# An attention and bilinear-FFN kernel: GpSimd copies patterns by 64-bit additions, VectorE takes the norm multiplications and 175 key tiles, and the order is planned anew

## The chip, the cores and the metric

One core of a Trainium2 chip. Its engines run their own instruction queues: TensorE (PE, with its weight loads listed as PEld), VectorE (DVE), ScalarE (ACT), GpSimd (POOL), and SyncE (SP), which here only starts DMA transfers. They meet through semaphores. Everything one engine does is in program order on that engine.

The metric is the device time of the program in microseconds (us), one launch on one core. The kernel before takes 706.86 us, the median of three runs between 705.78 and 707.62.

## What is computed

Two branches over the same 2048 rows of 512 values, mixed row by row by a sigmoid gate:

```python
def _A_ref(x, wqkv, wo):            # S = 2048, D = 512, H = 32 heads, Dh = 16
    qkv = (x @ wqkv).reshape(B, S, 3, H, Dh).transpose(2, 0, 3, 1, 4)
    q, k, v = qkv[0], qkv[1], qkv[2]
    scores = einsum("bhqd,bhkd->bhqk", q, k) * (Dh ** -0.5)
    p = softmax(scores, axis=-1)
    o = einsum("bhqk,bhkd->bhqd", p, v)
    return o.transpose(0, 2, 1, 3).reshape(B, S, D) @ wo

def _B_ref(x, w_gate, w_up, w_down):     # F = 1376
    return ((x @ w_gate) * (x @ w_up)) @ w_down

g = sigmoid((x * gate_w).sum(-1, keepdims=True))
out = g * _A_ref(x, ...) + (1 - g) * _B_ref(x, ...)
```

The heavy part is the softmax: 32 heads x 2048 x 2048 exponentials, 134 million.

## The kernel before

**Tiles.** The queries are cut into four chunks of 512, the heads into groups of eight. A "quad" is four heads with one chunk of queries: 32 quads, taken one after the other. For each quad there are 16 key tiles of 128 keys, so 512 steps in all. A step has four score tiles, each 128 keys by 512 queries, one PSUM bank each. Each bank is made by four matmuls that use one half of the PE array (64 rows) and a quarter of its columns each; the two halves work side by side (`scores` and `pe64`, L1621, where every such matmul is recorded). The banks then go one of two ways.

- An **A step**: ACT takes the exponential of a bank, or of two neighbouring banks in one instruction, and writes bf16 weights to SBUF cells (`exp`, L1721). Then 8 matmuls multiply the four cells with the values (`pv`).
- A **D step**: VectorE approximates the exponential. One addition and a clamp per bank turn the scaled score into a 16-bit integer whose bits, read as bf16, are a piecewise-linear power of two (`dpass`, L1757). To average out the error of that shape there are four patterns: the integers themselves and three copies with 32, 64 and 96 added (`copy`, L1763 on VectorE, L1767 on GpSimd). Each pattern is multiplied with the values scaled by 2^(-v/4), prepared by `v_scale`, so that a D step has 32 value matmuls and not 8. A copy is 128 x 2048 16-bit numbers, or half of that.

Six of the 16 key tiles of a quad (`dks`) may be D steps; 150 of the 512 steps are.

**Value sums and norm.** All value matmuls of a quad add up in PSUM bank 7; a seventeenth column of ones gives the denominators. At the end of a quad VectorE moves the bank out, scaled by a row of gate factors (L1833). For each pair of quads the denominators are gathered by a DMA, inverted (`recip`, L1847), written to DRAM and read back broadcast to all rows (`rbc`, L1918). A multiplication on GpSimd, `mult` (L1926), then gives the normed block. 16 of these are recorded.

**Filling.** The projections for keys, values and queries, the FFN (`u_copy`, `g_mul`) and the output projection are cut into units of a few matmuls on one bank and put between the attention steps.

**The order.** Nothing in the order is left to a run-time scheduler. `_Sched` is a planner that plays the program through with its own durations for each instruction and appends each instruction to its engine's list as it chooses it. In `try_act`, `try_dve`, `try_pool` and `pe_phase` it asks a set of knobs (`PAR`), each a table over planned time with an entry per 4 us: how many score banks may be out, when ACT waits for a neighbouring bank, when GpSimd and when VectorE copies. `_Plan.emit` then writes the lists out, with a semaphore wait wherever an instruction needs another engine's result. The planner lets VectorE's copies and GpSimd's instructions exclude each other (`lock_v`, `dve4_until`), and a GpSimd copy also waits for the last of VectorE's (`last4`).

**Buffers.** The patterns live in eight buffers `DB` and, after their first use as weights, in `wv` and `wk`; the ACT cells in `PT`, and later in `xT`, `wd`, `wu`, `wg`, `hT` and `wo` as these come free.

Of the kernel before, what the change touches and what calls it, by code (L numbers as in the profile page):

```python
# [10 lines left out]
I32 = mybir.dt.int32  # L11
# [126 lines left out]
class _Sched:  # L138
# [582 lines left out]
    def try_act(self):  # L721
# [27 lines left out]
        if grp is not None and self.cfree[grp]:  # L749
            n = 1  # L750
            if len(self.cfree[grp]) > 1:
                for i in range(len(rd)):
                    j = next((j for j in range(i + 1, len(rd)) if abs(rd[j][4] - rd[i][4]) == 1), None)
                    if j is not None and (i == 0 or self.g("apick")):
                        x, y = rd[i], rd[j]
                        rd.remove(x)
                        rd.remove(y)
                        rd[:0] = [x, y]
                        n = 2
                        break  # L760
                if n == 1 and o == 2:
                    n = 0
                if n == 1 and o != 1 and any(abs(x[4] - rd[0][4]) == 1 and x[0] <= self.now + self.g("await") for x in self.aready):
                    n = 0
        for x in rd[n:]:
            heapq.heappush(self.aready, x)
        if n == 0:
            return False
        rd = rd[:n]
        cells = [self.cfree[grp].pop(0) for _ in range(n)]  # L770
# [27 lines left out]


# [5 lines left out]
    def try_dve(self):  # L805
# [18 lines left out]
        for x in self.small:  # L824
            if x[0] <= now:
# [3 lines left out]
                return True  # L829
        c4 = self.lock_v <= now  # L830
# [102 lines left out]
    def cp_done(self, e, v, hs, op, t):  # L933
# [6 lines left out]
        if not e.cptodo:  # L940
            self.cpq.remove(e)
        if st[5] == 2:
# [30 lines left out]
    def try_pool(self):  # L973
# [5 lines left out]
        for x in self.ptask:  # L979
            if x[0] <= now:  # L980
                self.ptask.remove(x)
                self.log("pool", x[1], x[3])
                self.pool_v = self.lock_v = self.now + x[1]
                self.at(self.pool_v)
                x[2]()
                return True
        if self.dve4_until + 0.063 > now:
            return False
        if self.accq and self.accq[0][2] <= now:
            self.acc_pool()  # L990
            return True
        for e in self.cpq:
# [127 lines left out]
    def norm1(self, m, op):  # L1120
# [48 lines left out]
    def norm2(self, bi):  # L1169
# [21 lines left out]
    def norm3(self, bi, o):  # L1191
        c, b = divmod(bi, 4)
        op = self.hw.mult(bi, [o] + self.dep([("x", ch) for ch in range(1, min(self.par["xq"], 2) + 1)]) + self.rdep(("ocb", bi)) + [self.last4] + self.rdep(("outl", c - 2))) if self.hw else None
        self.setr(("ot", bi), self.now + 1.27 + 0.05 + 0.05, op)
# [261 lines left out]
    def run(self):  # L1456
# [29 lines left out]
        self.oev, self.fev, self.small, self.cpq, self.scale4, self.ptask = [], [], [], [], [], []  # L1486
# [63 lines left out]
class _Hw:  # L1550
# [6 lines left out]
    def __init__(self, nc, stack, par, A_x, A_wqkv, A_wo, W_gate, W_up, W_down, gate_w, out):  # L1557
# [42 lines left out]
        self.cadd = sb("cadd", [128, 4, 2], I16)  # L1600
# [111 lines left out]
    def exp(self, banks, cells, deps):  # L1712
        g, i = cells[0]
        t = self.grp[g]
        if len(banks) == 2:
            s = cells[1][1] - i
            dst = t[:, i : cells[1][1] + 1 : s, :]
            src = self.ps[:, banks[0] : banks[1] + 1, :]
# [40 lines left out]
    def copy(self, eng, src, dst, v, hs, deps):  # L1759
        lo, hi = 1024 * hs[0], 1024 * hs[-1] + 1024  # L1760
        a, o = self.db[src][:, lo:hi], self.db[dst][:, lo:hi]
        if eng == "dve":
            return self.dve(lambda e: e.tensor_scalar(o, a, 32.0 * v, None, ALU.add), deps)  # L1763
        n = (hi - lo) // 2
        return self.P.op(
            "pool",
            lambda e: e.tensor_tensor(o.bitcast(I32), a.bitcast(I32), self.cadd[:, v, :].bitcast(I32).to_broadcast([128, n]), ALU.add),  # L1767
            deps + [self.r["cadd"]],
        )
# [144 lines left out]

    def rbc(self, bi, deps):
# [9 lines left out]
    def mult(self, bi, deps):  # L1925
        return self.P.op("pool", lambda g: g.tensor_tensor(self.OT[:, bi % 8, :], self.oc[:], self.rb[:], ALU.mult), deps)  # L1926


    def prologue(self):
# [55 lines left out]
        for v in range(1, 4):  # L1985
            ca = pool(lambda g, v=v: g.memset(self.cadd[:, v, :], 32.0 * v))
# [60 lines left out]
        r["cadd"] = ca  # L2047
        r["qmz"] = qz2
        if self.par["acc"]:
# [9 lines left out]
 'ND': 8,  # L2059
 'acc': 0,  # L2060
# [3 lines left out]
 'alook': ((13, 2), (5, 6), (8, 4), (6, 2), (9, 6), (6, 2), (3, 4), (8, 2), (2, 6), (2, 5), (3, 6), (6, 5),  # L2064
           (4, 2), (3, 5), (15, 2), (3, 6), (5, 2), (7, 6), (2, 2), (15, 6), (3, 3), (24, 2), (12, 6), (6, 2),
           (10, 5)),
 'alook2': ((8, 4), (5, 3), (1, 4), (3, 6), (1, 4), (5, 3), (9, 0), (5, 5), (21, 4), (10, 6), (10, 4), (2, 3),
            (3, 0), (8, 4), (1, 6), (3, 5), (9, 6), (6, 4), (18, 5), (21, 4), (6, 5), (9, 0), (16, 6)),
 'amax': ((7, 5), (157, 4), (6, 5), (10, 4)),
 'amin': ((7, 3), (1, 2), (7, 3), (5, 2), (3, 3), (2, 2), (1, 4), (6, 2), (6, 4), (3, 3), (3, 4), (13, 2),  # L2070
          (2, 4), (9, 3), (10, 2), (2, 4), (13, 2), (8, 4), (9, 2), (18, 4), (25, 2), (5, 4), (6, 3), (6, 2),
          (10, 3)),
 'apick': ((11, 0), (17, 1), (52, 0), (3, 1), (6, 0), (17, 1), (55, 0), (3, 1), (16, 0)),
 'ares': ((14, 1), (9, 2), (9, 1), (5, 2), (1, 1), (3, 2), (3, 0), (14, 1), (10, 0), (10, 2), (2, 1), (11, 2),
          (13, 1), (6, 0), (15, 2), (15, 0), (15, 2), (15, 1), (10, 0)),
 'await': ((2, 0.05), (10, 0), (6, 0.05), (5, 0), (3, 0.2), (6, 0.1), (5, 0.2), (1, 0), (3, 0.05), (3, 0),
           (12, 0.05), (2, 0), (1, 0.1), (3, 0.4), (6, 0), (10, 0.05), (2, 0), (3, 0.2), (6, 0.05), (5, 0.1),
           (16, 0), (18, 0.2), (12, 0), (6, 0.05), (3, 0.2), (9, 0.05), (6, 0.4), (6, 0.2), (10, 0.4)),
 'cpmax': ((2, 10), (12, 6), (3, 4), (6, 6), (8, 5), (1, 8), (5, 14), (1, 5), (3, 8), (3, 14), (3, 8),
           (11, 14), (6, 3), (7, 14), (4, 5), (3, 14), (2, 10), (3, 8), (8, 5), (4, 6), (45, 14), (10, 5),  # L2080
           (3, 14), (2, 10), (6, 14), (3, 8), (3, 5), (3, 10), (10, 3)),
 'dact': ((13, 2), (24, 3), (4, 2), (3, 3), (14, 2), (79, 3), (8, 2), (19, 3), (6, 1), (10, 3)),
 'dahead': ((2, 0), (56, 1), (10, 0), (21, 1), (5, 0), (73, 1), (13, 0)),
 'dend': ((2, 2), (3, 3), (2, 1), (10, 0), (20, 3), (4, 5), (3, 0), (6, 2), (18, 4), (3, 3), (4, 4), (3, 3),
          (2, 0), (12, 4), (3, 0), (15, 2), (3, 5), (6, 3), (3, 5), (3, 0), (3, 3), (12, 2), (3, 3), (9, 4),
          (6, 3), (6, 4), (6, 2), (10, 4)),
 'dks': [2, 4, 7, 9, 12, 14],
# [3 lines left out]
 'dlook': ((29, 1), (8, 2), (7, 1), (6, 0), (51, 1), (4, 2), (5, 1), (18, 2), (24, 1), (6, 2), (3, 1), (3, 2),  # L2091
           (16, 1)),
 'dlook2': ((2, 0), (6, 1), (11, 0), (4, 3), (9, 2), (3, 4), (6, 1), (6, 3), (11, 2), (10, 3), (12, 0),
            (3, 3), (8, 0), (5, 3), (8, 2), (6, 3), (3, 4), (6, 1), (9, 4), (12, 3), (13, 0), (1, 3), (3, 4),
            (1, 0), (12, 1), (10, 3)),
 'dmaq': 2.0,
 'dmax': ((5, 2), (3, 3), (24, 2), (12, 3), (6, 2), (30, 3), (3, 2), (8, 3), (10, 2), (79, 3)),
 'dpair': ((8, 1), (3, 2), (17, 0), (1, 1), (3, 2), (9, 0), (27, 1), (3, 2), (9, 0), (3, 1), (11, 0), (1, 2),
           (15, 1), (15, 0), (3, 2), (12, 1), (18, 0), (6, 2), (16, 1)),
 'dpri': ((21, 1), (29, 0), (9, 1), (105, 0), (6, 1), (10, 0)),  # L2100
 'dresv': ((8, 0), (5, 3), (79, 0), (9, 1), (79, 0)),
 'dwait': ((2, 0.4), (3, 0), (20, 0.2), (1, 0.1), (6, 0.2), (5, 0.4), (1, 0.2), (3, 0), (3, 0.1), (11, 0),
           (10, 0.1), (3, 0.4), (9, 0.2), (3, 0.1), (11, 0.2), (4, 0), (15, 0.1), (18, 0.4), (9, 0.1),
           (9, 0.2), (6, 0.1), (6, 0), (6, 0.4), (6, 0), (10, 0.1)),
 'fcf': ((7, 1), (173, 0)),
 'fdebt': ((2, 0), (9, -10), (3, 25), (3, 0), (11, 25), (2, 0), (2, -30), (5, 25), (1, 0), (3, -30), (17, 25),
           (2, 10), (11, 0), (7, 25), (2, 0), (3, -30), (8, 25), (1, 0), (14, -30), (4, 25), (3, 10), (6, 25),
           (6, 10), (15, 25), (8, 0), (7, 25), (9, 0), (6, -30), (10, 0)),
 'ffn0': 2.6,
 'ffn1': 31.5,  # L2110
 'flead': ((2, 160), (3, 40), (6, 160), (6, 10), (12, 0), (9, 80), (3, 160), (12, 10), (9, 160), (4, 20),
           (2, 40), (3, 10), (9, 80), (3, 40), (8, 80), (1, 160), (9, 10), (9, 20), (18, 80), (9, 20), (3, 0),
           (5, 20), (8, 80), (1, 160), (1, 80), (9, 0), (6, 80), (10, 160)),
 'fmax': ((41, 3), (17, 1), (8, 2), (5, 3), (9, 2), (3, 3), (8, 2), (19, 1), (18, 3), (14, 1), (11, 2),
          (11, 3), (6, 1), (10, 2)),
# [116 lines left out]
```

## Time and profile before

| what | value |
|---|---|
| median of three runs | 706.86 us (705.78 to 707.62) |
| span of the profiled execution | 702.0 us |
| granted clock of TensorE, mean | 0.999 |
| PE busy, matmuls | 688.9 us, 22,151 |
| ACT busy | 681.2 us |
| DVE busy | 652.3 us |
| POOL busy | 460.4 us |
| HBM traffic | 20 GB/s over the span |

The profiled execution is told by its span, from the first to the last instruction; the runs' times also hold what lies before and after. A busy time is the union of an engine's instructions. An instruction's record begins before the one ahead of it has ended, since each engine overlaps the end of one with the start of the next, so the price of an instruction in a full queue is the step from its start to the next one's. A matmul is 0.38 us long in the record, while eight are under way at a time. The listing of a group gives line, engine, operation, output and inputs with shapes, then count, busy time, mean duration, and the idle time of the engine just before, with what ended it.

### The profile page before, as it was taken

The page shows a single profiled execution, that of the slowest core. Times are in us where ns is not written, and L with a number is a line of the kernel's source. Part 1 is how long each engine was busy: PE and PEld are TensorE (multiplying, and loading weights), DVE is VectorE, ACT ScalarE, POOL GpSimd, SP SyncE. Part 2 cuts the span into 40 slices and gives each one's busy share as a digit, 9 for nine tenths or more (in the row PEclk, how much of TensorE's full clock was granted, in tenths as well). Part 3 has the DMA queues.
Part 4 walks back from the last instruction along what each step waited for, and adds up shares of the span by engine and source line. Part 5 has one row for each costly group of instructions (what it writes and reads, how often), then busy time and mean ns, then how long its engine had stood idle before and what let it go on. Part 6 is the DMA issues. An engine that isn't in the chain of part 4 may idle for free.

```text
span 702.0 us, 47197 instructions
## 1 busy us (share of the span) xinstructions
PE 688.9 (98%) x22151; PEld 370.6 (53%) x22151; DVE 652.3 (93%) x1063; ACT 681.2 (97%) x839; POOL 460.4 (66%) x328
## 2 busy tenths in 40 slices
PE   8999999999999999999999999999999999999997
PEld 4565555455444545555544555555554555555564
DVE  5899999999999999999999999899999988999986
ACT  5899999999999999999999999999999999999995
POOL 3348877777765657777675566777776576768711
PEclk9999999999999999999999999999999999999999
DMA  7301341103010100001000010100101010010101
GB/s 153 74 4 47 97 100 28 14 13 101 17 29 12 43 12 21 28 12 28 14 21 20 21 33 19 35 13 12 29 5 42 13 36 22 10 29 19 30 20 34
DMA packets 33748, 22.94 MB, mean 33 GB/s; under 512 B 19500, under 2 KB 30156, under 8 KB 33552
## 3 DMA queue, kind: packets, MB, share of 16 engines
q1 hardware_dynamic: 32416, 18.86, 10.9%
q8 instruction: 173, 2.83, 1.7%
q0 software_dynamic: 176, 0.53, 0.3%
q10 hardware_dynamic: 960, 0.52, 0.3%
q14 instruction: 23, 0.19, 0.1%
HBM read 11.71 MB, written 2.36 MB: 20 GB/s over the span
## 4 chain that ended last, share of the span: by engine, by line
PE 71%; ACT 26%; DVE 1%; DMA 1%; issue 0%; ACTq 0%; DVEq 0%
PE ps L1621 70%; ACT PT L1721 16%; ACT xT L1721 8%; ACT wd L1721 2%; DMA DB<-in_A_x_dram 1%; ACT wu L1721 1%; DVE DB L1757 0%; DVE hT L1905 0%; ACT wg L1721 0%; PE ps L2020 0%; DVE oraw L1833 0%; DVE wv L1757 0%; ACTq L1936 0%; ACT QM L2033 0%; DVEq L88 0%
## 5 line engine op out<-in xcount | busy, mean ns | idle before, releaser
L1621 PE MATMUL ps<-QM,KT 64*32 64x512 bf16 x8192 | 497.2, 379 | 3.4 <-ACT wd L1721 0.8
L1721 ACT ACTIVATE PT<-ps 128x1024 bf16<-128x1024 f32 (+1 forms) x449 | 404.3, 1049 | 1.8 <-PE ps L1621 1.8
L1767 POOL TENSOR_TENSOR DB<-DB,cadd 128x1024 int32<-128x1024 int32 (+1 forms) x186 | 279.0, 1519 | 141.5 <-DVE DB L1763 56.2
L1757 DVE TENSOR_SCALAR DB<-ps 128x512 int16<-128x512 f32 (+1 forms) x457 | 304.8, 694 | 21.8 <-PE ps L1621 16.7
L1621 PE MATMUL ps<-DB,Vs 64*17 64x512 bf16 x3024 | 275.6, 377 | 0.5 <-issue 0.3
L1621 PEld LDWEIGHTS ps<-QM,KT 64*32 64x32 bf16 x8192 | 155.0, 90 | 162.5 <-ACT PT L1721 51.1
L1621 PE MATMUL ps<-PT,Vp 64*17 64x512 bf16 x1638 | 227.5, 377 | 0.2
L1721 ACT ACTIVATE xT<-ps 128x1024 bf16<-128x1024 f32 (+1 forms) x232 | 211.4, 1028 | 0.9 <-PE ps L1621 0.8
L1621 PE MATMUL ps<-xT,Vp 64*17 64x512 bf16 x822 | 145.9, 377 | 0.1
L1621 PE MATMUL ps<-xT,wu 64*32 64x512 bf16 x1376 | 110.5, 377 | 0.0
L1621 PE MATMUL ps<-xT,wg 64*32 64x512 bf16 x1376 | 108.2, 377 | 0.0
L1621 PE MATMUL ps<-wd,hT 64*32 64x512 bf16 x1408 | 102.2, 377 | 0.0
L1763 DVE TENSOR_SCALAR DB<-DB 128x2048 int16<-128x2048 int16 (+1 forms) x140 | 95.9, 714 | 0.5 <-PE ps L1621 0.2
L1621 PEld LDWEIGHTS ps<-DB,Vs 64*17 64x17 bf16 x3024 | 74.1, 87 | 34.0 <-PE ps L1621 5.1
L1621 PE MATMUL ps<-DB,Vp 64*17 64x512 bf16 x928 | 89.7, 377 | 0.8 <-DVE oraw L1833 0.3
L1621 PEld LDWEIGHTS ps<-PT,Vp 64*17 64x17 bf16 x1638 | 56.6, 87 | 21.0 <-PE ps L1621 7.2
L1721 ACT ACTIVATE wd<-ps 128x1024 bf16<-128x1024 f32 (+1 forms) x73 | 66.1, 1058 | 0.0
L1767 POOL TENSOR_TENSOR DB<-wv,cadd 128x512 int32<-128x512 int32 (+1 forms) x35 | 50.0, 1452 | 21.6 <-PE ps L1621 15.3
L1757 DVE TENSOR_SCALAR wv<-ps 128x512 int16<-128x512 f32 (+1 forms) x78 | 52.7, 699 | 2.5 <-PE ps L1621 1.7
L1621 PEld LDWEIGHTS ps<-wd,hT 64*32 64x32 bf16 x1408 | 36.8, 92 | 13.0 <-issue 1.2
L1621 PEld LDWEIGHTS ps<-xT,wu 64*32 64x32 bf16 x1376 | 35.5, 92 | 13.3 <-DVE DB L1757 1.0
L1621 PEld LDWEIGHTS ps<-xT,wg 64*32 64x32 bf16 x1376 | 34.8, 92 | 13.5 <-DVE DB L1757 1.3
(108 smaller groups left out, 890.9 us busy)
## 6 DMA issues: line engine op xcount, KB each, us to landing
rb<-rscr SPq DMA_DIRECT2D x16, 256.0 KB
QM<-qraw SPq DMA_DIRECT2D x124, 16.0 KB, 2.2
oc<-oraw SPq DMA_DIRECT2D x60, 32.0 KB, 2.3
out_dram<-ost SPq DMA_DIRECT2D x12, 128.0 KB, 2.2
wd<-in_B_w_down_dram SPq DMA_DIRECT2D x10, 128.0 KB, 2.3
wu<-in_B_w_up_dram SPq DMA_DIRECT2D x12, 96.0 KB, 3.1
wg<-in_B_w_gate_dram SPq DMA_DIRECT2D x12, 96.0 KB, 2.1
wv<-in_A_wqkv_dram POOLq DMA_DIRECT2D x1, 512.0 KB, 4.8
```

Source lines behind the costliest of these rows:

```text
L1621: o = pe.matmul(dst, lhs, rhs, start=st, stop=sp, tile_position=(64 * r, 32 * cc), skip_group_check=True)
L1721: return self.P.op("act", lambda a: a.activation(dst, src, ACT.Exp, scale=self.ES), deps)
L1757: return self.dve(lambda v: v.tensor_scalar(dst, src, self.YB, 0.0, ALU.add, ALU.max), deps)
L1763: return self.dve(lambda e: e.tensor_scalar(o, a, 32.0 * v, None, ALU.add), deps)
L1767: lambda e: e.tensor_tensor(o.bitcast(I32), a.bitcast(I32), self.cadd[:, v, :].bitcast(I32).to_broadcast([128, n]), ALU.add),
```

## The change

- GpSimd's copies: `copy` for "pool" was a 32-bit tensor addition with a constant tile `cadd`, broadcast, as second operand. It becomes `int64_add` with an immediate, 0x0020002000200020 times v, over the same bytes seen as 64-bit integers. `cadd` and its three memsets go. The operation belongs to another GpSimd code library than the one loaded at the start, and the program's listing has a load of it ahead of the first copy. A new function `turn`, a GpSimd addition over the small `mask` tile, is issued when the last copy is planned; ahead of it the first library is loaded again.
- The norm multiplication `mult` goes from GpSimd to VectorE. In the planner it has a queue of its own, `mq`, looked at after the small tasks and before the copies and passes; it counts as an instruction that excludes GpSimd's, as VectorE's copies do.
- The planner may give ACT three banks at equal distances of cells in one instruction (`three`, knob `a3`), and charges other durations: a GpSimd copy 1.02 and half a copy 0.593, where it had 1.849 and 0.997; the reciprocal 0.27, where it had 0.58.
- All knob tables are new. In the listing this makes 175 D steps (150 before), 1037 exponentials over one bank, 154 over two and one over three (204, 622 and none before), 55 whole copies and one half on VectorE (219 and 12), 415 whole and 109 half copies on GpSimd (156 and 138), and 22,751 matmuls (22,151).

```diff
+        if self.mq and self.mq[0][0] <= now:
+            x = self.mq.pop(0)
+            dur = 0.602 + max(0.0, self.lock_v - self.now)
+            self.dve_go(dur, ("M", x[1]))
+            self.dve4_until = self.dve_v + 0.165
+            (self.at(self.dve4_until), self.at(self.dve4_until + 0.063))
+            self.norm3(x[1], x[2], dur)
+            return True
...
         if not e.cptodo:
             self.cpq.remove(e)
+            if self.hw and self.qd >= self.NG and all(x.npass == 4 and not x.cptodo for x in self.dsteps[-6:]):
+                self.hw.turn()
...
             if both and bl >= self.g("gfull"):
-                hs, dur = [0, 1], 1.849
+                hs, dur = [0, 1], 1.02
             elif bl >= self.g("ghalf"):
-                hs, dur = [h], 0.997
+                hs, dur = [h], 0.593
...
-                self.small.append((t + self.par["rmarg"], 0.58, lambda: self.norm2(bi), ("R", bi)))
+                self.small.append((t + self.par["rmarg"], 0.27, lambda: self.norm2(bi), ("R", bi)))
...
-                    self.ptask.append((t2 + self.par["mmarg"], 1.27, lambda: self.norm3(bi, o2), ("M", bi)))
+                    self.mq.append((t2 + self.par["mmarg"], bi, o2))
...
-        n = (hi - lo) // 2
-        return self.P.op(
-            "pool",
-            lambda e: e.tensor_tensor(o.bitcast(I32), a.bitcast(I32), self.cadd[:, v, :].bitcast(I32).to_broadcast([128, n]), ALU.add),
-            deps + [self.r["cadd"]],
-        )
+        return self.P.op("pool", lambda e: e.int64_add(o.bitcast(I64), a.bitcast(I64), 0x0020002000200020 * v), deps)
...
+    def turn(self):
+        return self.P.op("pool", lambda g: g.tensor_tensor(self.mask[:], self.mask[:], self.mask[:], ALU.add), [self.r["q"], self.r["q0b"]])
...
     def mult(self, bi, deps):
-        return self.P.op("pool", lambda g: g.tensor_tensor(self.OT[:, bi % 8, :], self.oc[:], self.rb[:], ALU.mult), deps)
+        return self.dve(lambda v: v.tensor_tensor(self.OT[:, bi % 8, :], self.oc[:], self.rb[:], ALU.mult), deps)
...
-        for v in range(1, 4):
-            ca = pool(lambda g, v=v: g.memset(self.cadd[:, v, :], 32.0 * v))
...
 PAR = {'NA': 14,
  'ND': 8,
+ 'a3': ((4, -1), (2, 0.1), (6, -1), (2, 0.1), (1, 0.4), (2, -1), (2, 0.1), (1, 0.05), (11, -1), (1, 0.05), (5, 0),
...
- 'await': ((2, 0.05), (10, 0), (6, 0.05), (5, 0), (3, 0.2), (6, 0.1), (5, 0.2), (1, 0), (3, 0.05), (3, 0),
...
+ 'await': ((3, 0.05), (1, 0), (2, 0.1), (2, 0.05), (1, 0.1), (2, 0.2), (6, 0), (2, 0.05), (26, 0), (2, 0.1), (3, 0),
...
```

More of the change, by code (lines that the diff above doesn't have):

```diff
@@ L10 @@
 I16 = mybir.dt.int16
-I32 = mybir.dt.int32
+I64 = mybir.dt.int64
 ACT = mybir.ActivationFunctionType
@@ L764, in try_act @@
                     n = 0
+        cells = None
+        a3 = self.g("a3")
+        if n == 2 and a3 >= 0:
+            lo = min(rd[0][4], rd[1][4])
+            cells = self.three()
+            if cells:
+                j = next((j for j in range(2, len(rd)) if rd[j][4] in (lo - 1, lo + 2)), None)
+                if j is not None:
+                    rd.insert(2, rd.pop(j))
+                    n = 3
+                elif any(x[4] in (lo - 1, lo + 2) and x[0] <= self.now + a3 for x in self.aready):
+                    n = 0
+                else:
+                    cells = None
+        if n == 0:
+            for x in rd:
+                heapq.heappush(self.aready, x)
+            return False
         for x in rd[n:]:
             heapq.heappush(self.aready, x)
-        if n == 0:
-            return False
         rd = rd[:n]
-        cells = [self.cfree[grp].pop(0) for _ in range(n)]
+        if n == 3:
+            for x in cells:
+                self.cfree[x[0]].remove(x)
+        else:
+            cells = [self.cfree[grp].pop(0) for _ in range(n)]
         cells.sort()
@@ L797, in try_act, with three @@
         return True
+    def three(self):
+        for gi in (8, 9, 10, 1, 2, 7, 6, 5, 4, 3, 0):
+            f = self.cfree[gi]
+            if len(f) < 3:
+                continue
+            c = sorted(x[1] for x in f)
+            for i in range(len(c) - 2):
+                for j in range(i + 1, len(c) - 1):
+                    if 2 * c[j] - c[i] in c:
+                        return [(gi, c[i]), (gi, c[j]), (gi, 2 * c[j] - c[i])]
+        return None
     def dve_go(self, dur, what):
@@ L1189, in norm2, with norm3 @@
         self.at(t, go)
-    def norm3(self, bi, o):
+    def norm3(self, bi, o, dur):
         c, b = divmod(bi, 4)
-        op = self.hw.mult(bi, [o] + self.dep([("x", ch) for ch in range(1, min(self.par["xq"], 2) + 1)]) + self.rdep(("ocb", bi)) + [self.last4] + self.rdep(("outl", c - 2))) if self.hw else None
-        self.setr(("ot", bi), self.now + 1.27 + 0.05 + 0.05, op)
+        op = self.hw.mult(bi, [o] + self.dep([("x", ch) for ch in range(1, min(self.par["xq"], 2) + 1)]) + self.rdep(("ocb", bi)) + self.rdep(("outl", c - 2))) if self.hw else None
+        self.last4 = op
+        self.setr(("ot", bi), self.now + dur + self.DEND + 0.05, op)
     def simple(self, dur, dend, key, make, after=None):
@@ L1485, in run @@
         self.dma_v = 0.0
-        self.oev, self.fev, self.small, self.cpq, self.scale4, self.ptask = [], [], [], [], [], []
+        self.oev, self.fev, self.small, self.cpq, self.scale4, self.mq = [], [], [], [], [], []
         self.fact, self.fnext, self.fdone = [], 0, 0
@@ L1714, in exp @@
         t = self.grp[g]
-        if len(banks) == 2:
+        if len(banks) > 1:
             s = cells[1][1] - i
-            dst = t[:, i : cells[1][1] + 1 : s, :]
-            src = self.ps[:, banks[0] : banks[1] + 1, :]
+            dst = t[:, i : cells[-1][1] + 1 : s, :]
+            src = self.ps[:, banks[0] : banks[-1] + 1, :]
         else:
@@ L2046, in prologue @@
         r["er1"] = er1
-        r["cadd"] = ca
         r["qmz"] = qz2
@@ new lines @@
+ 'fmax': ((12, 3), (2, 2), (1, 3), (8, 2), (6, 3), (9, 2), (1, 3), (2, 1), (1, 2), (8, 1), (13, 3), (1, 2), (19, 3),
+          (1, 1), (2, 3), (3, 2), (21, 3), (5, 2), (3, 3), (1, 1), (2, 2), (1, 1), (1, 3), (1, 1), (4, 3), (1, 1),
+          (1, 2), (1, 1), (25, 3), (6, 1), (1, 3), (2, 1)),
+ 'fres': ((130, 0), (1, 1), (30, 0), (1, 2), (1, 0), (1, 1), (1, 0)),
+ 'fs2': ((10, 1), (2, 0), (2, 1), (5, 0), (1, 1), (6, 0), (5, 1), (7, 0), (89, 1), (1, 0), (12, 1), (1, 0), (17, 1),
+         (5, 0), (2, 1)),
@@ L2135 @@
+ 'gwin': ((1, 0), (3, 0.5), (2, 0), (3, 0.5), (2, 0), (1, 0.8), (2, 0), (5, 0.2), (7, 0.8), (3, 1.2), (2, 0.2),
[5 rows of a table added]
  'hold': 1,
```

140 lines of the change are left out of this document (58 added, 82 removed), and 67 rows, old and new, of the table PAR.

## The prediction

> **What bounds the kernel now.** I read the page's first and fourth parts, then the groups by form, the waits, the stages and the timeline. The page:
>
> ```profile
> span 702.0 us, 47197 instructions
> PE 688.9 (98%) x22151; PEld 370.6 (53%) x22151; DVE 652.3 (93%) x1063; ACT 681.2 (97%) x839; POOL 460.4 (66%) x328
> ...
> PE 71%; ACT 26%; DVE 1%; DMA 1%; issue 0%; ACTq 0%; DVEq 0%
> ...
> L1721 ACT ACTIVATE PT<-ps 128x1024 bf16<-128x1024 f32 (+1 forms) x449 | 404.3, 1049 | 1.8 <-PE ps L1621 1.8
> ```
>
> Three engines are over 90% busy and the chain changes between PE and ACT, so busy shares don't say which one binds. An instruction's busy time also overlaps the next one's, so I price by the step between starts. The timeline (start, length, engine and group):
>
> ```profile
> 304.05 0.64 ACT L1721 ACTIVATE xT<-ps 128x512 bf16<-128x512 f32 x1
> 304.53 1.76 ACT L1721 ACTIVATE PT<-ps 128x512 bf16<-128x512 f32 x3
> ...
> 328.32 4.80 ACT L1721 ACTIVATE PT<-ps 128x1024 bf16<-128x1024 f32 x5
> 332.90 2.05 ACT L1721 ACTIVATE xT<-ps 128x1024 bf16<-128x1024 f32 x2
> ```
>
> An exponential over one bank takes 0.48 us, one over two banks 4.58/5 = 0.916. The program before lists 204 and 622 of them: 97.9 + 569.8 = 667.7 us. They run from 9.57 (the chain) to 692.0 (the stages of line 1721 alone):
>
> ```profile
> 9.57 3.35 ACT wu L1721 x4
> ```
>
> ```profile
> 10.00:692.00 682.00, 673.73 (x826) 1.00 0.12 30
> 692.00:702.00 10.00, 0.00 (x0) 0.91 0.16 54
> ```
>
> So ACT works 667.7 of 682.4 us, 97.8%, and loses 14.7 us: ACT is the bound. PE has room. The stages, with the number of matmuls behind each busy time:
>
> ```profile
> core 0: us, PE busy (x) PEld busy (x) DVE busy (x) ACT busy (x) POOL busy (x), PEclk, DMA share, GB/s
> 0.00:20.00 20.00, 17.14 (x327) 9.62 (x327) 12.19 (x26) 12.44 (x19) 6.52 (x15) 1.00 0.77 145
> ...
> 60.00:160.00 100.00, 98.78 (x3216) 51.80 (x3208) 94.47 (x153) 99.64 (x114) 77.21 (x45) 1.00 0.22 52
> 160.00:260.00 100.00, 99.51 (x3032) 48.95 (x3023) 96.81 (x156) 99.41 (x123) 65.11 (x57) 1.00 0.13 36
> ...
> 560.00:660.00 100.00, 99.59 (x3388) 57.52 (x3384) 94.22 (x147) 99.45 (x116) 72.36 (x49) 1.00 0.08 22
> ```
>
> A PE "99% busy" does 3032 matmuls in one stage and 3388 in another: 33.0 and 29.5 ns each. Four matmuls on one half of the array start every 0.215 us when nothing holds them:
>
> ```profile
> 687.82 0.39 PE L1621 MATMUL ps<-wd,hT 64*32 64x512 bf16 x4
> 688.03 0.39 PE L1621 MATMUL ps<-wd,hT 64*32 64x512 bf16 x4
> 688.25 0.39 PE L1621 MATMUL ps<-wd,hT 64*32 64x512 bf16 x4
> ```
>
> With both halves that is 0.215/8 = 26.9 ns each. What holds PE is mostly ACT, which frees the score banks (the waits):
>
> ```profile
> PEld ps L1621 <- ACT PT L1721: 51.7, 207, 0.8
> ...
> PEld ps L1621 <- ACT xT L1721: 26.9, 112, 0.5
> ...
> PEld ps L1621 <- DVE DB L1757: 16.0, 70, 0.6
> ```
>
> **The change, part by part.** Counts are from the listings of the two programs, durations from the profiled execution.
>
> *25 more key tiles on VectorE (150 to 175 of 512).* ACT loses 100 of 1448 banks. The new order however takes few in pairs: 1037 of one bank, 154 of two, one of three. Cost 497.8 + 141.1 + 1.4 = 640.3 us (the three-bank one as two steps), 27.4 less than now.
>
> PE gets 24 matmuls per tile, 600: 22,151 to 22,751. At today's 31.1 ns (0.1 ms stage, x3216) that would be 18.7 us if PE bound; beside ACT it costs nothing while PE can run denser than it does.
>
> *Pattern copies.* 450 become 525. VectorE made 219 whole and 12 half, now 55 and one half; GpSimd 156 whole and 138 half, now 415 and 109. Their rows, and what else GpSimd's durations depend on:
>
> ```profile
> L1767 POOL TENSOR_TENSOR DB<-DB,cadd 128x1024 int32<-128x1024 int32 x105 | 196.8, 1891 | 96.7 <-DVE DB L1763 39.5 <-PE ps L1621 31.2 <-DVE DB L1757 17.0
> ...
> L1767 POOL TENSOR_TENSOR DB<-DB,cadd 128x512 int32<-128x512 int32 x81 | 82.3, 1037 | 44.8 <-DVE DB L1763 16.7 <-PE ps L1621 14.5 <-DVE wv L1763 7.4
> ```
>
> ```profile
> 2.27 0.52 POOL L1960 MEMSET erow<- 128x512 f32 x1
> 2.73 0.95 POOL L1961 MEMSET QM<- 128x1024 bf16 x1
> ...
> 20.89 3.74 POOL L1767 TENSOR_TENSOR DB<-DB,cadd 128x1024 int32<-128x1024 int32 x2 [11.66 <-DVE DB L1757]
> ```
>
> No row has a 64-bit addition. A whole copy is 1024 words of 32 bits, or 512 of 64. If elements count it costs what 512 do, 1.04; if bytes count, 1.89; if one operand instead of two is what matters, down to the memset's 0.52. The memsets, of 2 KB both, take 0.52 and 0.95 for 512 and 1024 elements, so elements count: I take 1.04 whole and, with 0.85 us per 512 elements (1.89 - 1.04), 0.61 half. GpSimd then works 415 x 1.04 + 109 x 0.61 = 498 us, 74% of the forecast's 669; it stays off the path, and a pattern is ready sooner.
>
> The Trainium skill (GPSIMD Engine Reference, section 3.1) has two-input bodies at about 2.6 cycles per element and small one-input bodies at 1.03, with a 1.2 GHz clock. 1024 words at 1.03 cycles would be an estimated 0.88 us plus dispatch, close to the 1.04 I take; the sum would not move.
>
> *VectorE.* Its steps:
>
> ```profile
> 318.90 1.28 DVE L1763 TENSOR_SCALAR DB<-DB 128x2048 int16<-128x2048 int16 x2
> 320.10 0.35 DVE L1847 RECIPROCAL rec<-den 128x32 f32<-128x32 f32 x1
> ...
> 323.18 1.28 DVE L1757 TENSOR_SCALAR wv<-ps 128x512 int16<-128x512 f32 x2
> 324.38 1.29 DVE L1763 TENSOR_SCALAR DB<-DB 128x2048 int16<-128x2048 int16 x2
> ```
>
> ```profile
> L1757 DVE TENSOR_SCALAR DB<-ps 128x1024 int16<-128x1024 f32 x7 | 8.5, 1219 | 1.0 <-PE ps L1621 0.8
> ...
> L1763 DVE TENSOR_SCALAR DB<-DB 128x1024 int16<-128x1024 int16 x3 | 1.3, 419 | 0.0
> ```
>
> Both a score pass and a whole copy take 0.60 (two in 1.20, start to start). Passes go from 582 (and 9 double, 1.2) to 692 (and 4): +60 us. Copies go from 219 to 55, and 11 of 12 halves (0.42 at most) go: -103 us. The 16 norm multiplications come over from GpSimd:
>
> ```profile
> L1926 POOL TENSOR_TENSOR OT<-oc,rb 128x512 bf16<-128x512 f32 x16 | 20.5, 1279 | 28.2 <-DVE DB L1763 28.2
> ...
> L1882 DVE TENSOR_TENSOR OT<-oraw,rb 128x256 bf16<-128x256 f32 x2 | 0.8, 424 | 0.3 <-ACT rb L1881 0.3
> ```
>
> The half-size form takes 0.42 on VectorE, so 0.42 to 0.85 whole; with 0.60 that is 9.6 us. Together VectorE does 33 us less. The multiplication reads two SBUF tiles; if VectorE must wait out a GpSimd copy each time, 16 x 1.04 = 16.6 us come back, still under today's load. What is new is a wait in VectorE's queue for the broadcast reciprocals (line 1947, by DMA). Behind it stand score passes of 0.6 us each, and PE waits for the banks they free. Before, GpSimd waited for that transfer once:
>
> ```profile
> POOL DB L1767 <- DMA rb<-rscr: 2.0, 1, 2.0
> ```
>
> Bounds: 0 to 16 x 2.0 = 32 us. I take 0, nearest to one in sixteen, since the 28.2 us in which GpSimd's multiplications waited for VectorE show the reciprocals lying ready.
>
> *Two library loads on GpSimd* (the 64-bit addition lives in another one; the dummy addition of `turn` brings the first back). The one at the start is hidden by the 11.66 us before the first copy. The other falls into the idle before the tail's only GpSimd instruction:
>
> ```profile
> 697.95 1.26 POOL L1902 TENSOR_TENSOR hT<-oc,wu 128x512 bf16<-128x512 f32 x1 [10.30 <-DVE hT L1905]
> ```
>
> I price both at nothing; without that cover the first patterns come late, and PE's queue, in order, stands behind them. The `cadd` memsets and their dependency go, inside the same idle time. SP issues the same 370 instructions, in a new order; its transfers are cheap (a DMA share of 0.22 from 60 to 160 us, 0.13 from 160 to 260).
>
> **The sum.** Before the first exponential 9.6 us, after the last 10.0: both prologue and tail keep their work. Exponentials 640.3. ACT's loss is unknown: 0 if the order feeds it without a hole, and up to what PE's density sets. The chain's last matmuls:
>
> ```profile
> 696.64 0.48 PE ps L1621 x8
> ```
>
> At the best stage's 29.5 ns PE needs (22,751 - 327) x 29.5 = 661.5 us from 20.0 on, and 4.9 us follow its last matmul: 686.4. So the span lies between 659.9 and 686.4. Today's loss of 14.7 us would become 14.4 if it goes with the time ACT works (2.2% of 654.7), and 3.6 if it arises where two banks must be ready together (154 doubles for 622). A fuller PE speaks for the first, the single banks for the second; I take the middle, 9.0: 9.6 + 640.3 + 9.0 + 10.0 = 668.9. The median of the runs (706.86) is 4.9 us over the profiled span (702.0), which I add unchanged: 674.
>
> **The rivals.**
> PE becomes the bound at its best density: 686.4 + 4.9 = 691, faster. For it speaks that the forecast needs 28.7 ns for 644 us ((668.9 - 4.9 - 20.0)/22,424), which no stage reached; against it, that PE waits 79 us for ACT's banks, the very work that shrinks.
> PE can't run denser than on average: at 31.1 ns its 22,424 matmuls take 697.4 us, 722.3 + 4.9 = 727, slower. It decides from 30.2 ns ((702.0 - 24.9)/22,424). The stage at 29.5 speaks against it.
> The 64-bit addition costs by bytes, so that the change doesn't do what it says: 415 x 1.89 + 109 x 1.04 = 898 us on GpSimd alone, with 21 before and about 15 behind it 934 + 4.9 = 939, slower. From some 1.4 us a copy GpSimd's 667 us are full. The memsets speak against it.
> The library load isn't hidden: it begins only with the first copy. Should it last as long as the whole idle stretch, all behind it moves by 11.7: 686. The Trainium skill (GPSIMD Engine Reference, section 2.1) puts the first call after a load at about 6 us, which no row here shows; by it the time would be an estimated 680 without cover.
>
> **How the numbers follow.** Forecast 0.62 (own range 665 to 686), PE at its best density 0.21, the load 0.04; slower: PE's mean density 0.06, bytes 0.04. The 0.03 left is for the others' neighbourhood within 0.3%, about what a measurement of this kernel tells from no change. Faster 0.87, same 0.03, slower 0.10. The range goes from 662, the span's lower bound of 659.9 with half of the 4.9, to 694, past the second case.
>
> **What would show it.** Right: GpSimd's new group at about 1.04 us per whole copy and under 80% busy; ACT's step at 0.48 and its exponentials ending some 10 us before the end; matmuls at 3450 or more per 100 us; fewer PE waits for ACT. Wrong: PE waits for GpSimd's copies as their longest entry, VectorE idle for the reciprocals' DMA, stages of 3200 matmuls, or an idle GpSimd stretch behind the first data.

## The result and the profile after

The changed kernel takes 697.77 us, the median of four runs between 695.81 and 700.59; the kernel before, in the same session, 707.24. The ratio is 0.988 (0.9847 to 0.9914): 1.2% faster, where 674 us, 4.6%, was forecast. The profiled execution took 700.59 us with a span of 698.8. Ratios, here and below, leave disturbed runs out; medians and ranges keep them.

The page of the changed kernel (busy time by engine; the queue of instruction fetches; the chain that ended last; GpSimd's new group as count, busy, mean ns, idle before and its releaser):

```profile
span 698.8 us, 48944 instructions
PE 680.9 (97%) x22751; PEld 391.3 (56%) x22751; DVE 618.4 (88%) x1009; ACT 671.2 (96%) x1205; POOL 498.4 (71%) x540
...
q8 instruction: 178, 2.92, 1.8%
...
PE 93%; ACT 3%; issue 2%; DMA 1%; POOL 0%; DVE 0%; SPq 0%; DVEq 0%
...
L1795 POOL INT64_ADD DB<-DB x350 | 327.4, 949 | 146.7 <-PE ps L1652 76.7
```

The chain says it first. ACT had 26% of it and PE 71%; now PE has 93%. VectorE is 34 us less busy, and GpSimd works 498 us. The forecast had the same 498, but for the copies alone; they take 488.8, and 9.8 go to GpSimd's other instructions, so that the match is luck. All that was meant to become lighter on ACT and VectorE did. The stages of the changed kernel, with the number of matmuls behind PE's busy time:

```profile
60.00:160.00 100.00, 98.00 (x3302) 56.78 (x3294) 91.71 (x150) 97.53 (x179) 82.94 (x97) 1.00 0.21 50
160.00:260.00 100.00, 98.73 (x3378) 57.90 (x3370) 86.95 (x139) 97.63 (x159) 73.33 (x79) 1.00 0.15 41
260.00:360.00 100.00, 99.02 (x3312) 54.06 (x3292) 93.76 (x150) 98.78 (x186) 88.96 (x96) 1.00 0.07 17
...
560.00:660.00 100.00, 97.92 (x3453) 58.47 (x3438) 88.94 (x143) 98.01 (x195) 66.73 (x72) 1.00 0.08 21
```

Up to 660 us PE is denser than before in every stage, but only the last of these reaches the 3450 that I had asked for; it is at 100/3453 = 29.0 ns per matmul, the usual one at 30. What stops it stands in the waits (total, times, longest):

```profile
PEld ps L1652 <- issue: 43.7, 93, 1.5
DVE DB L1788 <- PE ps L1652: 43.5, 98, 1.8
PEld ps L1652 <- DVE DB L1788: 25.3, 120, 0.5
...
PEld ps L1652 <- ACT PT L1752: 15.3, 67, 0.7
PEld ps L1652 <- ACT xT L1752: 14.7, 60, 0.5
...
POOL mask L1942 <- issue: 7.0, 1, 7.0
```

The waits for ACT fell from 78.6 us to 30.0, as forecast. In their place PE's weight loads wait 43.7 us for "issue", that is, for nothing that the profile shows. The kernel before has that row too, and I had passed over it:

```profile
PEld ps L1621 <- issue: 10.3, 26, 1.7
```

Where these gaps lie, the chain of the changed kernel in order of time shows (start, length, what; here from 74 to 94 us):

```profile
74.17 3.86 PE ps L1652 x126
78.03 0.14 issue
78.17 3.85 PE ps L1652 x128
82.02 0.15 issue
82.17 3.66 PE ps L1652 x128
85.83 0.35 issue
86.18 3.78 PE ps L1652 x128
89.96 0.22 issue
90.18 3.85 PE ps L1652 x128
```

A gap after every 128 matmuls; the rows of PE start some 4.0 us apart. It is so all through the kernel: from 25 us on every weight load that waits more than 0.15 us for "issue" stands a multiple of 128 loads behind the one before it, give or take two. Each matmul has its own weight load, so 128 of them are 256 instructions. The q8 row agrees: 178 transfers of 2.92 MB are 16.4 KB each, and 2 x 22,751 PE instructions in 178 portions are 255.6. Every run below fits that too. So PE's program comes in blocks of 256 instructions. In the trace a block's transfer begins about 1.2 us after PE has crossed into the block ahead of it, and PE goes on 2.2 to 2.9 us after that; the transfer itself is the smaller part, 0.9 to 1.5 us. The 59 blocks of the changed kernel that lie between two such gaps lasted 3.46 to 4.84 us, 3.87 in the mean, or 30 ns per matmul, while the array would need 128 x 26.9 = 3.44 us.

The Trainium skill (Runtime: NRT & Kernel Launch, section "Instruction fetch mechanics") also describes refills in blocks of 256 instructions, and has the crossing of a block border mostly hidden. The first half agrees with the trace; the second doesn't for PE here: 93 waits and 43.7 us at 178 blocks.

### The profile page after: what moved, and what is told of

It reads as the page before. It is cut to its first block, busy times and chain, and to the rows that moved or that the text cites. A ratio compares the mean times of both kernels' runs of the same rounds, so it can differ in the third digit from the quotient of the medians.

```text
span 698.8 us, 48944 instructions
## 1 busy us (share of the span) xinstructions
PE 680.9 (97%) x22751; PEld 391.3 (56%) x22751; DVE 618.4 (88%) x1009; ACT 671.2 (96%) x1205; POOL 498.4 (71%) x540
## 3 DMA queue, kind: packets, MB, share of 16 engines
q8 instruction: 178, 2.92, 1.8%
## 4 chain that ended last, share of the span: by engine, by line
PE 93%; ACT 3%; issue 2%; DMA 1%; POOL 0%; DVE 0%; SPq 0%; DVEq 0%
PE ps L1652 93%; ACT PT L1752 1%; DMA wv<-in_A_wqkv_dram 1%; ACT xT L1752 1%; DMA wk<-in_A_wqkv_dram 1%; ACT wg L1752 0%; ACT wo L1752 0%; ACT hT L1752 0%; DVE hT L1931 0%; ACT wu L1752 0%; POOL DB L1795 0%; POOL wv L1795 0%; POOL wq L1891 0%; SPq L1965 0%; DVEq L88 0%
## 5 line engine op out<-in xcount | busy, mean ns | idle before, releaser
L1652 PE MATMUL ps<-QM,KT 64*32 64x512 bf16 x8192 | 573.9, 378 | 2.8 <-issue 0.9
L1788 DVE TENSOR_SCALAR DB<-ps 128x512 int16<-128x512 f32 x592 | 390.6, 689 | 48.0 <-PE ps L1652 43.5
L1795 POOL INT64_ADD DB<-DB x350 | 327.4, 949 | 146.7 <-PE ps L1652 76.7
L1752 ACT ACTIVATE PT<-ps 128x512 bf16<-128x512 f32 (+1 forms) x588 | 354.3, 720 | 6.1 <-PE ps L1652 4.3
L1652 PEld LDWEIGHTS ps<-QM,KT 64*32 64x32 bf16 x8192 | 204.5, 91 | 134.9 <-DVE DB L1788 24.4
L1752 ACT ACTIVATE xT<-ps 128x512 bf16<-128x512 f32 (+1 forms) x392 | 241.5, 726 | 3.5 <-PE ps L1652 2.7
L1752 ACT ACTIVATE wd<-ps 128x512 bf16<-128x512 f32 (+1 forms) x132 | 75.7, 685 | 2.3 <-PE ps L1652 1.6
L1795 POOL INT64_ADD wv<-DB x52 | 50.7, 978 | 4.9 <-PE ps L1652 2.4
L1795 POOL INT64_ADD wk<-DB x43 | 43.1, 1004 | 7.7 <-DVE DB L1788 4.5
L1788 DVE TENSOR_SCALAR wv<-ps 128x512 int16<-128x512 f32 x64 | 42.3, 684 | 5.2 <-PE ps L1652 4.9
```

The lines of the kernel that those rows point to most:

```text
L1652: o = pe.matmul(dst, lhs, rhs, start=st, stop=sp, tile_position=(64 * r, 32 * cc), skip_group_check=True)
L1752: return self.P.op("act", lambda a: a.activation(dst, src, ACT.Exp, scale=self.ES), deps)
L1788: return self.dve(lambda v: v.tensor_scalar(dst, src, self.YB, 0.0, ALU.add, ALU.max), deps)
L1795: return self.P.op("pool", lambda e: e.int64_add(o.bitcast(I64), a.bitcast(I64), 0x0020002000200020 * v), deps)
```

## The experiments

The theory, F: PE can't go through its instructions faster than 128 matmuls in about 3.73 us, whatever the array needs. Its rivals are that the array is full (A), and that the order alone sets the time. The changed kernel's own executions lie between 692.7 and 700.8 us, so a difference of a few us between two single executions says nothing.

**1. The instruction stream by itself.** A kernel in which PE issues nothing but matmuls that wait for nobody:

```python
for k in range(160):
    for r in (0, 1):
        small(wa, r, k, 512)   # four 64x32 matmuls over 512 columns
# (cut here) the same over 256 and over 128 columns;
# then 640 matmuls of 64x128; then both shapes in turn: 2 wide and 8 small, later 16 and 64
```

> A kernel of nothing but matmuls, with no wait between them; the whole computation is left out and zeros are written. Three stretches of 1280 small matmuls as in the kernel (64 rows by 32 columns, eight side by side) over 512, 256 and 128 columns, then 640 matmuls of 64 rows by 128 columns over 512, then two stretches that mix both shapes (a change of shape every two or eight, and every 16 or 64). Theory F: PE's instructions come in 16 KB blocks of 256 (128 weight loads with 128 matmuls), and no block can begin less than about 3.7 us after the one before it. Then each of the first three stretches (10 blocks) takes about 37 us, whatever its columns. Rival A: the array's own time sets PE's pace. Then they take 34, 17 and 9 us. The wide stretch takes 68 us by both (320 steps of 0.2133). The mixed ones take 34 us if a change of shape costs nothing, more by what it costs.

It took 283.8 us. Stretches of it (PE busy and count, PEld, VectorE, GpSimd, granted clock, DMA share, GB/s):

```profile
10.00:30.00 20.00, 20.00 (x752) 9.81 (x744) 0.00 (x0) 0.00 (x0) 1.00 0.02 5
...
41.00:48.70 7.70, 3.88 (x256) 3.45 (x256) 0.00 (x0) 0.00 (x0) 1.00 0.02 4
...
100.40:111.80 11.40, 5.72 (x384) 5.09 (x384) 0.00 (x0) 0.00 (x0) 0.50 0.02 4
```

And its chain between 41 and 49 us:

```profile
41.02 1.94 PE ps L45 x128
42.96 1.79 issue
44.74 1.94 PE ps L45 x128
46.68 2.06 issue
48.75 2.46 PE ps L45 x128
```

With 256 columns 128 pairs are through in 1.94 us, but the next 128 begin only 3.72 and 4.01 us after the ones before. With 128 columns, at half the granted clock, 384 take 11.40 us, 3.80 per block. From 41.03 to 111.86 us 19 blocks start 3.45 to 4.00 us apart, 3.73 in the mean. The distance follows neither the columns nor the clock; the border falls after exactly 128 pairs. The stretches over 256 and 128 columns take 37 us each, as F had it. So F holds there as a mean, not as a least time, and A doesn't.

The first stretch, over the kernel's own 512 columns, doesn't show the limit: its pairs run at 20.0/752 = 26.6 ns, which is A's pace, and its 36.5 us hold some 4 us at half the granted clock at the start. PE had a lead there and used it up: from 10.08 to 38.69 us the transfers of the blocks begin 3.58 us apart in the mean, while PE goes through a block in 3.45, and the chain has its first gap at 40.00.

Two by-products: a 64x128 matmul takes 70.4/640 = 0.110 us, about what four small ones do (4 x 26.6 ns = 0.106); and where the two shapes alternate every 2 and 8, the stretch takes 52 us instead of 34, about 0.115 us per change of shape. The group of the wide ones (count, busy, mean ns, idle):

```profile
L50 PE MATMUL ps<-x,wd 64*128 64x512 bf16 x640 | 70.4, 380 | 0.0
```

**2. Shorter matmuls, and fewer.** Both leave part of the value sums out, as said in the expectations:

```diff
-            mms.append((self.ps[32 * cc : 32 * cc + 17, 7, :], w, self.cell(cells[cc], lo, hi), first, True, cc))
+            n = 512 if first else 256
+            mms.append((self.ps[32 * cc : 32 * cc + 17, 7, 0:n], w, self.cell(cells[cc], lo, hi)[:, 0:n], first, True, cc))
```

> The changed kernel, in which all value matmuls but the first of a quad go over 256 of their 512 columns, so that half of the attention sums is left out. The number of instructions, their order and all waits stay; some 6,900 of 22,751 matmuls occupy the array for half as long, 6,800 x 0.107/8 = 90 us less array time. Theory F (instruction blocks, 128 pairs not faster than about 3.7 us): 688 to 700 us, as only the array got faster. Rival A (array time and full banks hold PE): 663 to 675, down to what ACT needs.

```diff
+            if v and cc == 3 and not first:
+                continue
```

> The changed kernel, in which the value matmuls of patterns 1 to 3 leave out one of their four column groups (one head in four lacks three of its four patterns on VectorE's tiles), save in the first job of a quad. The other three groups run as long as before, so the array's time per job is the same, but some 1,050 pairs of weight load and matmul are gone. Theory F: 1,050/128 = 8.2 blocks of 3.7 us less, 30 us: 665 to 675. Rival A: within 4 us of the changed kernel, 693 to 701.

Halving the columns of the value matmuls brought next to nothing: 697.5 us, span 695.8. PE's waits for ACT rose from 30.0 to 89.4 us, and the waits at block borders stayed:

```profile
PEld ps L1652 <- ACT PT L1753: 50.5, 189, 0.6
PEld ps L1652 <- issue: 50.3, 89, 1.8
...
PEld ps L1652 <- ACT xT L1753: 38.9, 130, 0.6
```

So the time that the array gave back went into waiting. Leaving out 1,050 matmuls out of groups of four that run side by side, so that the array is occupied as long as before, brought 19.2 us of span (16.4 by the runs' times): 681.42, span 679.6. As the order and ACT's work are the same in both, neither of these two alone had set the 697.5. The page and the waits of this second kernel:

```profile
q8 instruction: 169, 2.77, 1.8%
```

```profile
PEld ps L1652 <- ACT PT L1754: 42.8, 190, 0.4
PEld ps L1652 <- ACT xT L1754: 36.2, 157, 0.4
...
PEld ps L1652 <- issue: 13.7, 34, 1.3
```

In this kernel the time hangs on the number of instructions, not on the array's work. A missed in both; F's 665 to 675 for the second was too low, since 1,050/128 x 3.73 = 30.6 us went from PE and only 19.2 from the span. The rows say why: 30 of the 43.7 us of fetch waits went, and 49 us of waits for ACT came. Near 680 PE waits mostly for ACT again, as it did before the change.

**3. The engine parts without the new order.** The order of before, with the 64-bit copies, `turn`, and the norm multiplication on VectorE (150 tiles, 22,151 matmuls):

```diff
-            lambda e: e.tensor_tensor(o.bitcast(I32), a.bitcast(I32), self.cadd[:, v, :].bitcast(I32).to_broadcast([128, n]), ALU.add),
+        return self.P.op("pool", lambda e: e.int64_add(o.bitcast(I64), a.bitcast(I64), 0x0020002000200020 * v), deps)
...
-        return self.P.op("pool", lambda g: g.tensor_tensor(self.OT[:, bi % 8, :], self.oc[:], self.rb[:], ALU.mult), deps)
+        return self.dve(lambda v: v.tensor_tensor(self.OT[:, bi % 8, :], self.oc[:], self.rb[:], ALU.mult), deps)
```

> The kernel before with its own order and its 150 tiles, but with GpSimd's copies as 64-bit additions and the norm multiplication on VectorE: the two engine parts of the change alone. Theory F: PE's 22,151 pairs in the old order, and neither engine was ahead of PE or ACT in the chain: 700 to 708. Rival G: slow copies were what PE waited for in the old order: 680 to 695. Rival D: VectorE, waiting in its queue for the reciprocals' transfer or for GpSimd's port, delays PE: 710 to 725.

708.92 us beside 705.8 for the kernel before, ratio 1.0057 (1.0039 to 1.0076): 0.9 us above F's range and below the 710 at which D's begins. From 60 to 660 us GpSimd is busy 227 us where it was 421:

```profile
60.00:660.00 600.00, 594.60 (x19170) 313.53 (x19163) 569.25 (x923) 596.50 (x707) 227.19 (x279) 1.00 0.11 29
```

Half of GpSimd's work gone, and no gain: GpSimd bound nothing in the old order. So the gain of the change comes with the new order, which takes 25 tiles from ACT. That the cheap copies only make room for them is an inference; the new order was not run without them.

**4. Fewer instructions for the same work.** If the block is the limit, a score or filling job should be one 64x128 matmul and not four of 64x32. A new step ahead of the writing-out replaces the jobs of a run, if it is long enough; between the two shapes PE has to change twice per run.

```diff
+    def widen(self, least):
+        run = []
+        for o in [x for x in self.ops if x.eng == "pe"] + [None]:
+            if o is not None and o.wide is not None:
+                run.append(o)
+                continue
+            if len(run) >= least:
+                for x in run:
+                    x.fn = x.wide
+            run = []
...
+        o.wide = wide and (lambda pe: pe.matmul(wide[0], wide[1], wide[2], start=mms[0][3], stop=mms[0][4], tile_position=(64 * r, 0), skip_group_check=True))
...
+        hw.P.widen(6)
```

> The changed kernel with nothing left out and its order kept: wherever six or more jobs of scores or filling follow one another in PE's queue, with no value job between, the four matmuls of a job (64 rows by 32 columns each, same moving data) are one matmul of 64 by 128. 22,751 pairs become 20,742 and the array's work stays, but for 143 changes of shape at 0.115 us (the stretch that mixed both shapes took 18 us more than 34 for 160 of them), 16 us. Theory F: 2,009 pairs fewer are 15.7 blocks of 3.75 us, 59 us less time for instructions; ACT then bounds at 660 and what it loses: 670 to 684. Rival A (array time and full banks): 16 us more, 698 to 715.

With `widen(4)`:

> The same from four jobs in a row on: 19,019 pairs, 407 changes of shape, 47 us of array time. Theory F: the instructions need 557 us, the array 605 + 47 + some 25 at both ends = 677, so the array is now what is short: 678 to 692, no better than from six on. Rival A: 725 to 750.

The kernel before with `widen(6)`:

> The same from six jobs on in the kernel before: 22,151 pairs become 20,799, with 101 changes of shape, 12 us. There the waits for instructions were 10 us in all and ACT was the bound. Theory F: at most those 10 us, 694 to 703. Rival A: 12 us more, 708 to 720.

| kernel | matmuls | changes of shape | span of the profiled execution, us | median, us | ratio to before |
|---|---|---|---|---|---|
| changed | 22,751 | 0 | 698.8 | 697.77 | 0.988 (0.9847 to 0.9914) |
| runs of 6 and more | 20,742 | 143 | 692.8 | 696.45 | 0.9872 (0.9829 to 0.9916) |
| runs of 4 and more | 19,019 | 407 | 736.6 | 739.85 | 1.0496 (1.0445 to 1.0547) |
| before, runs of 6 and more | 20,799 | 101 | 711.6 | 713.02 | 1.0103 (1.007 to 1.0136) |

F's 670 to 684 for the first did not come, nor did its 678 to 692 for the second and its 694 to 703 for the kernel before; the last two lie in A's ranges (725 to 750 and 708 to 720). A change of shape costs array time by both theories, and F's ranges had it too cheap. The waits of the first show one reason (L1669 is the wide form, L1664 the small one):

```profile
PEld ps L1664 <- issue: 14.8, 37, 1.1
PEld ps L1669 <- issue: 14.0, 38, 0.4
```

The waits at block borders fell from 43.7 to 14.8, and the changes of shape took their place. An estimate of their price comes from the runs of 4 and of 6: 264 changes more for 736.6 - 692.8 = 43.8 us, 0.166 us each if the 1,723 matmuls fewer saved nothing and more if they did, against the 0.115 of the bare stream. 143 of them are 23.7 us, against 28.9 won at the borders. In the kernel before, with 10.3 us of block waits to win and 101 x 0.166 = 16.8 to pay, the time rose by 1%; there the block was no limit. The Trainium skill (TensorEngine Tiling (Array Packing), section "Key Properties") says that a change of tiling mode drains the engine; the runs here agree that a change costs time, 0.115 to 0.166 us.

**5. Wide only where it pays.** A run of n jobs saves 3n matmuls, up to 3n x 29 ns, and costs 2 x 0.166 us, so longer runs pay best. `widen(9)`:

> The changed kernel with the wide form (one 64x128 matmul in place of four 64x32) only in runs of nine score or filling jobs and more: 407 jobs in 33 runs, so about 1,220 pairs fewer than in the changed kernel and some 66 changes of shape, where the run with six and more had 2,009 and 143. Theory F (blocks of 128 pairs at 3.73 us, changes at 0.166 us, as the earlier runs gave them): 66 x 0.166 = 11 us are paid, and up to 1,220/128 x 3.73 = 35 us of fetch are saved where PE waits for blocks; ACT's own order sets in at a span of some 680 (the run with 1,050 pairs fewer). Between the best case of 682 and the rate of return of the run with six and more (29 of a possible 58 us of block waits went): 698.8 - 17 + 11 = 693, so 684 to 694 in time of the run. Rival A (the order alone sets the time, PE's form does not matter): 696 to 699.

`widen(12)`:

> The same with twelve jobs and more: 214 jobs in 13 runs, 642 pairs fewer and about 26 changes of shape. Theory F: 26 x 0.166 = 4.3 us paid, up to 642/128 x 3.73 = 18.7 saved, half of it as before: 698.8 - 9.4 + 4.3 = 693.7 in span, at best 684; 686 to 696 in time of the run. Rival A: 696 to 699.

The changed kernel beside them:

> The changed kernel itself beside the two, so that the three stand on one chip: 695.8 to 700.6, as measured before.

`widen(12)` once more, and `widen(16)`:

> The changed kernel with the wide form in runs of twelve jobs and more once more, since its four times lay between 686.5 and 698.4. Theory F: a median of 688 to 695. Rival A (the wide form brings nothing): 696 to 699, as the changed kernel itself.

> The same with sixteen and more: three runs, 81 jobs, 243 pairs fewer and about 6 changes of shape. Theory F: 243/128 x 3.73 = 7.1 us at the most less 6 x 0.166 = 1.0, half of it as before: 3 us less than the changed kernel, 693 to 697. Rival A: 696 to 699.

| runs of | matmuls | median and range, us | ratio to before |
|---|---|---|---|
| changed kernel again | 22,751 | 698.09 (692.7 to 703.61) | 0.9879 (0.9847 to 0.9911) |
| 9 and more | 21,530 | 693.01 (690.6 to 696.61) | 0.9842 (0.9788 to 0.9895) |
| 12 and more | 22,109 | 694.54 (686.54 to 698.37) | 0.9764 (0.9696 to 0.9831) |
| 12 and more, again | 22,109 | 692.54 (689.21 to 695.55) | 0.9815 (0.9781 to 0.9849) |
| 16 and more | 22,508 | 699.31 (696.05 to 702.64) | 0.9909 (0.9873 to 0.9945) |

The ratio in the third row rests on two of its four times, so the repetition is the better figure. The repeated kernel's waits:

```profile
PEld ps L1664 <- issue: 26.3, 58, 2.0
PEld ps L1664 <- ACT PT L1769: 22.7, 104, 0.4
PEld ps L1664 <- ACT xT L1769: 18.8, 81, 0.4
...
PEld ps L1669 <- issue: 3.0, 8, 0.4
```

With 642 matmuls fewer and some 26 changes the kernel is at 692.5 us, some 5 us under the changed kernel in the median, with intervals that only just touch; F had said 688 to 695. It and the version with 9 and more, which can't be told from it, are the fastest here; both medians lie in F's ranges (684 to 694 and 688 to 695), outside A's 696 to 699. The last version missed: 3 us were expected and none came; its block waits are still 37.1 us in the trace, against 38.3 to 43.7 in the two profiles of the changed kernel. I take it that such small savings depend on where they lie, since a block in which PE waits for ACT anyway gains nothing by being shorter; that was not tried.

## Why the prediction was wrong

The sign was right, the size and the bound were not: 674 was forecast with ACT as the bound, and 697.8, with PE having 93% of the chain, lies outside the range of 662 to 694. By the steps:

- *The failed step* is "beside ACT it costs nothing while PE can run denser than it does". The forecast needed 28.7 ns per matmul for 644 us, a block of 128 in 3.67 us. In the bare stream a block took 3.73 us in the mean, 29.1 ns a pair, and in the changed kernel 3.87 where PE waited at the border; the chain rows above show some 4.0. I took the 26.9 ns between matmuls late in the program as what PE can do; that is the array's figure over a few dozen matmuls, not the stream's. The best stage of before, 29.5 ns, is 3.78 us per block: the limit was in the quoted row already. "Which no stage reached", I wrote of the 28.7, and chose it all the same. With the 10.3 us of "issue" in the waits of before the cause could have been found. The limit alone doesn't make the whole miss: at 3.73 us a block the 22,409 matmuls after 20.0 us would take 653 us, and the span would be some 678. The other 20 us lie in blocks that lasted longer, and the waits of PE for ACT, VectorE and its own banks stand beside the block waits there; how they divide was not measured.
- *ACT's loss*, forecast at 9.0 within 3.6 to 14.4, is what this comes to: 698.8 - 9.1 - 640.3 - 8.8 = 40.6 us, with the first exponential at 9.1 and 8.8 us behind the last. Where the fetches are made fewer (experiment 2), 679.6 - 9.1 - 640.3 - 8.8 = 21.4 remain, if start and end are as here; so about 19 us of the 32 too many go with the fetches of 1,050 matmuls. The other 12 I can't split, and their cause stays open: some block waits remain there (13.7 us), and ACT and PE wait for each other.
- *The rival "PE becomes the bound at its best density"* had the bound and nearly the time, 691, though not the reason, the instruction blocks. It falls short since the mean over 60 to 660 us is 29.9 ns and not the best stage's 29.5, and since the last 39 us do 1,090 matmuls, 35.8 ns each. It had 0.21 of the chances and should have had the most. The rival at 31.1 ns was wrong, PE did run denser than on average.
- *The 64-bit copies* were right: 1.04 and 0.61 us were forecast. The timeline shows pairs of whole copies, start, length, and the idle time before:

```profile
24.24 2.06 POOL L1795 INT64_ADD DB<-DB  x2 [15.41 <-DVE DB L1794]
```

  Two are 2.06 us long, one start is 1.015 after the other, and a half takes 0.588. The price goes with the count of elements, not of bytes; that rival (939) is out. The operation went from two tensors to one and an immediate at the same time; that part was not measured by itself. GpSimd is 71% busy, under the 80% named ahead.
- *VectorE* lost 33.9 us of busy time (forecast: 33). The multiplication has no wait for the reciprocals' transfer, as priced at 0:

```profile
L1955 DVE TENSOR_TENSOR OT<-oc,rb 128x512 bf16<-128x512 f32 x16 | 12.4, 774 | 0.0
```

- *The library loads* cost nothing, as forecast: the first lies within the 15.41 us ahead of the first copy, where VectorE is named as the last releaser (its copy ends at 24.12, GpSimd's starts at 24.24), and the second shows as the 7.0 us of "issue" before `mask`, while the tail's work is still on PE. The Trainium skill (GPSIMD Engine Reference, section 2.1) has about 6 us for it; the 7.0 here may hold some waiting.
- *ACT's prices* were right: 0.478 us for one bank and 0.905 for two, against 0.48 and 0.916 (medians of the steps from start to start).
- *The 4.9 us* from span to time were a mistake of another kind. Span and time of one execution differ by 1.8 us (700.59 and 698.8); the rest of the 4.9 was that the profiled execution of before lay 3 us under the median. Of the error, 29.9 us in the span, the offset gave back some 6, since the profiled execution of after lies above its own median.

## What to carry to other kernels

Before a forecast lets PE run denser, count its instructions as well as its columns: with a weight load per matmul of 512 columns on a small tile, this core's instruction stream gave 128 pairs per 3.73 us in the mean once its lead was gone, however short the matmuls were. A wait that is put down to "issue" and comes back at equal distances is a resource without a row of its own; look for it before calling an engine free. And when a rate is needed that no stage of the trace has reached, forecast from the best stage, not from the midpoint to the ideal; here even that, 686.4, was 12 us short in the span.

## What the runs showed of the hardware that was not expected

- PE's instructions come in blocks of 256 (16.4 KB by the q8 rows), and in the bare stream 19 of them took 3.73 us each in the mean (3.45 to 4.00), at a granted clock of 1.00 as at 0.50. From the start to 40.00 us, some 1,300 pairs, the chain has PE without a gap; what sets that lead, and why it doesn't come back while PE waits for ACT, is left open.
- A change between matmuls of 64x32 and 64x128 costs PE 0.115 us in a bare stream and, by the difference of two runs, 0.166 us in the kernel. One 64x128 matmul takes as long as four of 64x32 side by side (0.110 and 0.106 us) with a quarter of the instructions.
- GpSimd's 64-bit addition with an immediate takes 1.015 us for 512 elements per row and 0.588 for 256, where the 32-bit addition of two tensors over the same bytes had 1.89 and 1.04.
